# Token-mixing MLP on one core: three pairs of unit blocks of the first product as seven block products over 12 of the 16 token rows, the half block first, early gelu results by way of DRAM

## The chip, the cores and the metric

The kernel runs on one NeuronCore of a Trainium2 chip. The metric is the device time of one execution in microseconds (us). Before the change three runs gave 671.99 us in the median (670.89 to 672.05). One further execution was recorded with a profile. Engines carry the profile's names: PE (TensorE, matmuls; PEld its weight loads), ACT (ScalarE), DVE (VectorE), POOL (GpSimd), SP (SyncE, which here issues nearly all DMAs). PSUM is the memory that PE writes its results to, SBUF the large on-chip memory.

## The reference

```python
h = _layernorm(x, axis=-1) * (1 + ca) + sa
x = x + ga * _A_ref(h, A_k, A_v, A_shift_k, A_ssm_k, A_ssm_D)   # short and long convolution along the tokens
h = _layernorm(x, axis=-1) * (1 + cb) + sb
# _B_ref(x, w1, b1, w2, b2): the MLP over the token axis
h = _layernorm(x, axis=-1)                     # (1, S=2048 tokens, D=640 channels)
u = jnp.einsum("bsd,sf->bdf", h, w1) + b1      # F=1728 hidden units
u = _gelu(u)
y = jnp.einsum("bdf,fs->bds", u, w2) + b2
x = x + gb * y                                 # y back in (1, S, D)
```

All data are fp32. The change lies in the first product, `u = gelu(w1^T h + b1)`.

## The kernel before

**Stages.** Up to about 290 us the kernel computes the convolution half. Then comes the MLP. The 2048 tokens lie as 16 rows `j` of 128 partitions, each with 640 channels; the 1728 units are 13 blocks of 128 and a half block of 64 (f = 13). fp32 accuracy on fp32r matmuls takes three products: a value is split into a high part (`H[j][0]`) and the rest (`H[j][1]`), a weight block likewise, and `mm` (L439) issues high x high, high x rest, rest x high, each for the two halves of 320 channels. A block is thus 16 rows x 3 steps x 2 halves = 96 matmuls of 128x320.

**Norm and products.** The loop over row pairs `pr` (0 to 7) normalises two rows (`root_in`, `root`, `halves`, `rests`, `norm1`, `second`) and multiplies them with unit blocks 0 to 3 (`products`, L784), which fill all four PSUM tiles.

**The other blocks.** Blocks 4 to 12 follow one after another (L957). `load_w` (L396) fetches a block ahead over SP, `split_w` (L424) makes its two parts on ACT (L434) and DVE, alternating between `wb0b` and `wb1b`. `u_evac` (L872) takes a finished PSUM tile: gelu in place on ACT (L877), then for each half an ACT copy of the high part (L887) and a DVE subtraction for the rest. The half block comes between blocks 5 and 6 (`half_block`, L908): plain fp32 on whole rows that `whole_rows` adds up again from high part and rest. All gelu results `U` stay in SBUF.

**The second product.** Its first four row blocks use the plain form (L1119, `U[0]` to `U[13]` in order). Twelve more are made pairwise as seven block products instead of eight (Winograd's form of Strassen's scheme; L1042). `t_ops` (L919) prepares sums of `U` for it; `t_ops(0)` to `t_ops(2)` stand ahead of `u_evac(12)`.

**What sets the order.** Each engine runs its instructions in the order in which the program text issues them. `psum()` hands out four tiles of 1024 fp32 (two halves of 512, of which 320 are used) in a ring; `mem(tag, n, name)` gives the SBUF region `tag` to a new use. Waits between engines are derived from what overlaps by a framework; DMAs of SP rotate through eight semaphores, so at most eight are outstanding.

Of the kernel before, what the change touches and what calls it, by code (L numbers as in the profile page):

```python
# [47 lines left out]
def mixer_kernel(ctx: ExitStack, tc: tile.TileContext, q, k, v, shift_k, ssm_k, ssm_D, w1, b1, w2, b2, c,  # L48
# [8 lines left out]
    TT = lambda eng, o, a, b, op: eng.tensor_tensor(o, a, b, op=op)  # L57
# [366 lines left out]
    def split_w(n, t2=None, eng=dve):  # L424
        if n >= len(order):
            return
        i = order[n]
# [4 lines left out]
        t, parts = raw.pop(i)
        for f in parts:
            act.activation(hi[:, f].bitcast(F32R), t[:, f], AF.Copy)  # L434
# [427 lines left out]
    U = {}  # L862
    thirds = lambda t, n, o=0: [t[:, o + 320 * i:o + 320 * i + 320] for i in range(n)]
    h_i, h_y = mem("in", 4288, "h_i"), mem("y", 4096, "h_y")
# [5 lines left out]
    us = [home(left[2 * f:2 * f + 2], right[2 * f:2 * f + 2]) for f in range(6)]  # L870

    def u_evac(f, ps):  # L872
        n = 25 - f if f > 11 else f
        u = U[f] = us[n] if n < 13 else [t[:, 320 * h:320 * h + 320] for t in H[15] for h in range(2)]
        if f < 13:
            p = [ps[:, h, 0:320] for h in range(2)]
            act.activation(ps[:, :, 0:320], ps[:, :, 0:320], AF.Gelu_apprx_tanh, bias=B1C[:, f:f + 1])  # L877
        else:
            p = [ps[64:128, 1, 0:320], ps[64:128, 0, 0:320]]
            for h in range(2):  # L880
                r = slice(64 * h, 64 * h + 64)
                act.activation(p[h], ps[r, 0, 0:320], AF.Gelu_apprx_tanh, bias=B1C[r, f:f + 1])
            for t_ in u:
                dve.memset(t_[0:64], 0.0)
            u = [t_[64:128] for t_ in u]
        for h in range(2):
            act.activation(u[h].bitcast(F32R), p[h], AF.Copy)  # L887
# [2 lines left out]
    m_p = mem("p", 2048, "m_p")
    HALF = 6
    w_half = m_p[:, 0:1024].rearrange("p (j m) -> p j m", j=16)
    whole = [t[:, 640 * i:640 * i + 640] for t, n in ((h_i, 6), (h_y, 6), (m_p[:, 1024:1664], 1)) for i in range(n)]
    whole = [(t[:, 0:320], t[:, 320:640]) for t in whole] + [(h_i[:, 3840:4160], m_p[:, 1664:1984])]
    whole += whole[0:2]

    def whole_rows(js):
        for j in js:  # L900
            if j != 13:
                o = whole[j][0]
                TT(dve, bass.AP(tensor=o.tensor, offset=o.offset, ap=[o.ap[0], [1, 640]]), *H[j], ALU.add)
            else:
                for h in range(2):
                    TT(dve, whole[j][h], *(t[:, 320 * h:320 * h + 320] for t in H[j]), ALU.add)

    def half_block(ps):  # L908

        for j in range(16):  # L910
            if j == 2:
                whole_rows((14, 15))
            for h in range(2):
                pe.matmul(ps[64 * h:64 * h + 64, 0, 0:320], w_half[:, j], whole[j][h], start=j == 0, stop=j == 15)  # L914
# [34 lines left out]
    T_wb = [mem("w0", 4096, "wb0b"), mem("w1", 4096, "wb1b")]
    u_evac(0, acc[0])  # L950
    split_w(4)
    load_w(5)
    for b in range(2):
        sync.dma_start(w_half[64 * b:64 * b + 64], dram(w1, 16 * b * F + 1664, [[32 * F, 64], [F, 16], [1, 64]]))
    for f_ in range(1, 4):
        u_evac(f_, acc[f_])
    for f_ in range(4, NF - 1):  # L957
        if f_ == HALF:
            ps = psum().rearrange("p (h m) -> p h m", h=2)
            half_block(ps)  # L960
            u_i, u_y = mem("in", 4288, "u_i"), mem("y", 4096, "u_y")
            us.append(home((thirds(u_i, 1, 3840) + thirds(r_z, 1, 7680)), right[12:14]))
            us += [thirds(t, 4, 1280 * i) for t in (u_i, u_y) for i in range(3)]
            u_evac(13, ps)
        ps = psum().rearrange("p (h m) -> p h m", h=2)
        split_w(f_ + 1)
        load_w(f_ + 2)
        if f_ < HALF:
            whole_rows(range(7 * f_ - 28, 7 * f_ - 21))
        for j in range(16):  # L970
            hh, hl = H[j]
            mm(ps, blk[f_][0][:, j], blk[f_][1][:, j], hh, hl, j == 0, j == 15)
        if f_ == NF - 2:
            m_v = mem("v", 4520, "m_v")
            for i in range(3):
                t_ops(i)
        u_evac(f_, ps)
# [210 lines left out]
```

## Time and profile before

| | |
|---|---|
| median of three runs | 671.99 us (670.89 to 672.05) |
| the profiled execution's own time | 675.24 us |
| its span (first to last instruction in the trace) | 673.5 us |
| mean granted TensorE clock | 0.98 |
| PE's share of the span | 93% |
| product loop for blocks 0 to 3, half block, blocks 4 to 12 | about 298 to 490 us |
| second product, plain form | 490 to 539 us |
| second product, seven products for a pair | 539 us to the end |

The trace lists each group of instructions as start, duration, engine, source line, operation, output<-inputs, shapes, count, and in brackets how long the engine stood idle ahead of it and who released it. Matmul ends are modelled; starts are recorded. 1.74 us of the execution lie outside the span (675.24 - 673.5).

### The profile page before, as it was taken

How to read it: one execution, taken by the hardware profiler on the slowest of the kernel's cores; microseconds unless marked ns; L12 is line 12 of the kernel's file. 1: busy time of each engine (PE TensorE's matmuls, PEld its weight loads, DVE VectorE, ACT ScalarE, POOL GpSimd, SP SyncE). 2: the span in 40 equal slices, each digit the busy share in tenths (PEclk: the TensorE clock that was granted, in tenths of full speed). 3: DMA queues.
4: the chain of work that ended last, by engine and by line, in shares of the span. 5: the costliest groups of instructions: out<-in, count | busy, mean ns of one | idle time of the engine just before them, and what ended most of it. 6: DMA issues, size and time to landing. Idle time of an engine off the chain costs nothing.

```text
span 673.5 us, 20730 instructions
## 1 busy us (share of the span) xinstructions
PE 628.8 (93%) x9115; PEld 597.2 (89%) x9115; DVE 498.5 (74%) x869; ACT 300.7 (45%) x483; POOL 127.1 (19%) x142
## 2 busy tenths in 40 slices
PE   6868878899999999879999999999999999999997
PEld 2868578889998997779899889999999999999997
DVE  7788778969899269789966622321589869888895
ACT  0564465736747456377764222322344143333331
POOL 5772038424126044000000000000000430000000
PEclk9999979999999799789999999999999999999999
DMA  9998998456525234160307433335342626346601
GB/s 177 217 242 232 319 178 165 103 88 144 98 66 178 66 98 151 33 141 19 63 1 130 90 64 63 63 63 118 113 134 68 195 80 184 116 138 168 187 33 38
DMA packets 166537, 81.22 MB, mean 121 GB/s; under 512 B 90830, under 2 KB 156912, under 8 KB 166448
## 3 DMA queue, kind: packets, MB, share of 16 engines
q1 hardware_dynamic: 159276, 78.32, 47.8%
q10 hardware_dynamic: 6916, 1.31, 1.2%
q8 instruction: 71, 1.16, 0.8%
q0 software_dynamic: 256, 0.28, 0.2%
q14 instruction: 18, 0.15, 0.1%
HBM read 69.40 MB, written 10.49 MB: 119 GB/s over the span
## 4 chain that ended last, share of the span: by engine, by line
PE 69%; DVE 16%; DMA 7%; issue 3%; ACT 3%; SPq 2%; ACTq 0%; DVEq 0%
PE pst L445 22%; PE pst L1042 16%; PE pst L1119 7%; PE pst L223 7%; PE pst L242 6%; PE pst L271 5%; PE pst L291 3%; DVE p L57 3%; DMA p<-in_w_mod_dram 2%; DMA in<-in_A_v_dram 2%; DMA v<-in_const_v_dram 1%; ACT z L280 1%; DVE tap L57 1%; PE pst L914 1%; DVE sm L548 1%
## 5 line engine op out<-in xcount | busy, mean ns | idle before, releaser
L242 PE MATMUL pst<-z,w 128*64 128x64 f32 x2560 | 78.6, 223 | 12.8 <-DVE p L57 6.6
L242 PEld LDWEIGHTS pst<-z,w 128*64 128x64 f32 x2560 | 76.5, 138 | 15.4 <-issue 11.0
L229 ACT ACTIVATE z<-pst 128x1024 f32<-128x1024 f32 (+2 forms) x45 | 43.0, 973 | 41.6 <-PE pst L223 41.5
L57 POOL TENSOR_TENSOR y<-p 128x256 f32<-128x256 f32 x72 | 51.3, 740 | 42.4 <-DVE p L57 42.1
L57 DVE TENSOR_TENSOR p<-pst,kt 128x512 f32<-128x512 f32 x80 | 50.9, 687 | 8.3 <-ACT kt L246 8.3
L57 POOL TENSOR_TENSOR m_p<-u_i,r_z 128x320 f32<-128x320 f32 x1 | 0.9, 874 | 263.9 <-DVE m_p L57 263.9
L271 PEld LDWEIGHTS pst<-v,y 32*128 32x128 f32 x1280 | 39.5, 192 | 5.4 <-issue 5.0
L271 PE MATMUL pst<-v,y 32*128 32x64 f32 x1280 | 41.5, 278 | 2.3 <-issue 2.2
L877 ACT ACTIVATE pst<-pst,sm 128x640 f32<-128x640 f32 x13 | 10.0, 766 | 71.6 <-PE pst L445 71.6
L1042 PE MATMUL pst<-r_z,m_w 128*128 128x320 f32 x222 | 41.6, 309 | 0.1
L223 PE MATMUL pst<-v,p 128*64 128x128 f32 x640 | 38.4, 281 | 1.9 <-ACT p L168 1.9
L246 ACT ACTIVATE kt<-pst 128x512 f32<-128x512 f32 x40 | 23.9, 598 | 34.6 <-PE pst L242 20.0
L223 PEld LDWEIGHTS pst<-v,p 128*64 128x64 f32 x640 | 36.4, 142 | 3.2 <-ACT p L168 2.7
L1030 ACT ACTIVATE m_w<-m_v 128x896 fp32r<-128x896 f32 x24 | 22.7, 951 | 31.5 <-PE pst L1042 16.8
L57 DVE TENSOR_TENSOR tap<-tap,kt 128x512 f32<-128x512 f32 x51 | 35.6, 697 | 1.3
L223 PE MATMUL pst<-v,x 128*64 128x128 f32 x512 | 34.4, 292 | 2.0 <-issue 1.5
L1042 PEld LDWEIGHTS pst<-r_z,m_w 128*128 128x128 f32 x222 | 34.8, 188 | 0.4 <-DVE m_w L57 0.4
L223 PEld LDWEIGHTS pst<-v,x 128*64 128x64 f32 x512 | 31.0, 147 | 3.2 <-issue 2.5
L291 PEld LDWEIGHTS pst<-z,v 64*64 64x64 f32 x1280 | 24.2, 157 | 9.0 <-issue 5.1
L280 ACT ACTIVATE z<-pst 128x512 f32<-128x512 f32 x38 | 20.9, 642 | 24.6 <-PE pst L271 24.6
L291 PE MATMUL pst<-z,v 64*64 64x64 f32 x1280 | 25.8, 242 | 6.1 <-issue 3.8
L57 DVE TENSOR_TENSOR m_w<-m_v,m_w 128x896 fp32r<-128x896 f32 x24 | 27.9, 1165 | 2.5 <-ACT m_w L1030 2.1
(306 smaller groups left out, 1496.0 us busy)
## 6 DMA issues: line engine op xcount, KB each, us to landing
x<-in_B_w_dram SPq DMA_DIRECT2D x20, 512.0 KB
m_x<-xs SPq DMA_DIRECT2D x28, 160.0 KB
out_dram<-m_x SPq DMA_DIRECT2D x28, 160.0 KB
aux<-in_A_ssm_k_dram SPq DMA_DIRECT2D x8, 512.0 KB
m_v<-in_B_w_dram SPq DMA_DIRECT2D x9, 448.0 KB
in<-in_w_mod_dram SPq DMA_DIRECT2D x4, 960.0 KB
x<-in_B_w_dram SPq DMA_DIRECT2D x7, 448.0 KB
in<-in_A_v_dram SPq DMA_DIRECT2D x22, 128.0 KB
```

Source lines behind the costliest of these rows:

```text
L57: TT = lambda eng, o, a, b, op: eng.tensor_tensor(o, a, b, op=op)
L223: pe.matmul(ps[64 * ri:64 * ri + 64, o:o + 255:2], lhs, F1[:, 128 * ri:128 * ri + 128], start=True, stop=True)
L229: act.activation(Z[:, side, t, :, k0:k1], ps.rearrange("p (a k e) -> p a k e", a=4, e=2)[:, :, k0:k1], AF.Copy)
L242: pe.matmul(ps[64 * h:64 * h + 64, o:o + 64], W2[k1 // 32][:, 2 * (k1 % 32) + ri], rhs, start=True, stop=True)
L246: act.activation(kt.rearrange("p (m i) -> p m i", i=32), pv[:, :, 1], AF.Copy)
L271: pe.matmul(pp[qd // 2][:, o:o + 64], Y[p, ri, i:i + 2].rearrange("p i k -> p (i k)"), V2[p, 64 * ri:64 * ri + 64], start=ri == 0, stop=ri ...
L280: act.activation(o, i, AF.Copy)
L291: pe.matmul(ps[64 * b:64 * b + 64, 512 * e + 64 * jj:512 * e + 64 * jj + 64], V1[p, ri, n2], T2[p, :, 32 * ri + n2], start=ri == 0, stop=r ...
L445: pe.matmul(ps[0:m, h, 0:320], w_.bitcast(F32R), r_[:, 320 * h:320 * h + 320].bitcast(F32R), start=first and i == 0, stop=last and i == 2)
L1030: act.activation(W[n][0].bitcast(F32R), A[p, w_], AF.Copy)
L1042: pe.matmul(bank[n], w[:, i].bitcast(F32R), r.bitcast(F32R), start=i == 0 and k == 0, stop=i == 6 and k == 2)
L1119: pe.matmul(acc[s][:, h, 0:320], w[:, f_].bitcast(F32R), u[r + h].bitcast(F32R), start=f_ == 0 and k == 0, stop=f_ == NF - 1 and k == 2)
```

## The change

Blocks 5 to 10 become three pairs. For a pair, 12 of the 16 rows form a two by two scheme: unit blocks f and f + 1; row groups `KA` (rows 0 to 3, 8, 9) and `KB` (rows 10 to 15); two halves of 320 channels. It is made as seven block products (`p_prod`: A11, A12, S1, S2, S4, S3, A22) of 6 rows x 3 steps = 18 matmuls. The remaining rows `KR` (4 to 7) take four plain products (`r_prod`) of 4 x 3 = 12. A pair is thus 7 x 18 + 4 x 12 = 174 matmuls in place of 192. Each product fills one half of a PSUM tile: a and b are the halves of one tile, c_ and d those of a second.

Around it: `fulls(pr)` keeps the normalised rows themselves (12 ACT operations of 128x640 in the product loop), since `x_sums` (12 DVE operations) builds sums of rows from them, and `x_parts` splits those (12 ACT copies, 13 DVE subtractions); for S3 and A22 this is done in `turns()` inside the first pair. Each weight tile (6 or 4 rows of w1) is loaded, summed (`w_sum`) and split (`w_parts`) by itself. The half block moves ahead of block 4. `U[0]` to `U[4]` and the row `GB` are written to DRAM (`away`, 21 DMAs) and fetched back ahead of the weights of the second product. Blocks 4, 11 and 12 keep the old form; `u_evac` and `t_ops` keep theirs too.

```diff
+    def fulls(pr):
+        for j in (2 * pr, 2 * pr + 1):
+            act.activation(row(j), row(j), AF.Identity, scale=at(R_, 2, j))
@@ product loop
+        if pr != 4:
+            fulls(pr - 2 if pr < 4 else pr - 1)
         rests(pr)
         products(pr)
@@ after it
+    def w_parts(key, t, hi, lo):
+        Ws[key] = hi, lo
+        act.activation(hi.bitcast(F32R), t, AF.Copy)
+        TT(dve, lo.bitcast(F32R), t, hi, ALU.subtract)
+    def w_split(p, w_, n=None):
+        w_parts((p, w_), tile_of(p, w_), *SL[(7 * p + (TYPES.index(w_) if n is None else n)) % 2])
+    def r_split(p, n):
+        w_parts((p, "R%d" % n), RT[2 * (p % 2) + n - 1], *RH)
+    half_ps = psum().rearrange("p (h m) -> p h m", h=2)
+    js = (0, 1, 10, 11, 2, 3, 12, 13, 8, 9, 4, 5, 6, 7, 14, 15)
+    for j in js:
+        for h in range(2):
+            pe.matmul(half_ps[64 * h:64 * h + 64, 0, 0:320], w_half[:, j], whole[j][h], start=j == js[0], stop=j == js[-1])
+    w_0 = mem("w0", 4096, "s_w0")
...
+            u = thirds(w_0, 4, 1280 * n)
+            u_evac(n + 1, acc[n + 1], u)
+            away(n + 1, u)
...
+    for p in range(3):
+        f = 5 + 2 * p
+        banks = [psum() for _ in range(2)]
+        a, b, c_, d = (t[:, 512 * h:512 * h + 320] for t in banks for h in range(2))
...
+        p_prod(a, p, "A11")
+        act.activation(v_, a, AF.Copy)
+        if p:
+            w_split(p, "A12")
+            w_sum(p, "S1")
+        r_prod(b, p, 1, 0, True, False)
+        w_split(p, "S1")
+        p_prod(b, p, "A12", False)
+        w_sum(p, "S3")
+        w_sum(p, "S2")
+        w_load(p + 1, "A11")
+        TT(dve, b, v_, b, ALU.add)
+        if p:
+            gelu(f, raws[f][0], b)
+        w_split(p, "S2")
+        w_sum(p, "S4")
+        w_load(p + 1, "A12")
+        p_prod(c_, p, "S1")
+        r_prod(d, p, 1, 1, True, False)
+        if p == 0:
+            x_r = turns()
+            gelu(f, raws[f][0], b)
+        w_split(p, "S4")
+        w_load(p + 1, "A21")
+        r_split(p, 2)
+        p_prod(a, p, "S2")
+        TT(dve, u_, a, v_, ALU.add)
+        TT(dve, v_, c_, u_, ALU.add)
+        w_split(p, "S3")
+        w_load(p + 1, "A22")
+        p_prod(d, p, "S4", False)
+        TT(dve, d, v_, d, ALU.add)
+        gelu(f, raws[f][1], d)
+        r_prod(b, p, 2, 1, True, True)
+        w_split(p, "A22")
...
+        p_prod(a, p, "S3")
+        TT(dve, u_, a, u_, ALU.add)
+        TT(dve, v_, c_, u_, ALU.add)
+        TT(dve, b, v_, b, ALU.add)
+        gelu(f + 1, raws[f + 1][1], b)
+        r_prod(d, p, 2, 0, True, False)
...
+        p_prod(d, p, "A22", False)
+        TT(dve, d, u_, d, ALU.add)
+        gelu(f + 1, raws[f + 1][0], d)
...
+    for f in range(5):
+        U[f] = us[f]
+        away(f, us[f], True)
...
+    load_w(13)
+    part(1, "2", ps, last=True)
```

The order in which PE's instructions stand shows what takes the place of a block. Before, block 6 reads (one row stands for several equal matmuls, given by the count at its end; `wb0b` holds the block's weight parts, `r_z`, `r_v`, `h_a` and `h_x` the rows' parts, `pst_127` is the PSUM tile):

```order
L445 MATMUL pst_127_5370<-r_z_4273,wb0b_5062 128x320 [waits Activation_49]
L445 MATMUL pst_127_5370<-r_z_4273,wb0b_5062 128x320 x17
L445 MATMUL pst_127_5370<-r_v_4274,wb0b_5062 128x320 x18
L445 MATMUL pst_127_5370<-h_a_4275,wb0b_5062 128x320 x12
L445 MATMUL pst_127_5370<-h_a_4275,wb0b_5062 128x320 [waits Activation_49]
L445 MATMUL pst_127_5370<-h_a_4275,wb0b_5062 128x320 x5
L445 MATMUL pst_127_5370<-r_z_4273,wb0b_5062 128x320 x18
L445 MATMUL pst_127_5370<-h_x_4879,wb0b_5062 128x320 x24
```

After, the second pair begins with A11 into half a of `pst_128` (the last 15 of its 18 matmuls are the first four rows here), then the first R product into half b of the same tile:

```order
L935 MATMUL pst_128_5554<-r_z_4273,s_w0_5141 128x320 x6
L935 MATMUL pst_128_5554<-r_v_4274,s_w0_5141 128x320 x3
L935 MATMUL pst_128_5554<-h_a_4275,s_w0_5141 128x320 x3
L935 MATMUL pst_128_5554<-r_z_4273,s_w0_5141 128x320 x3
L935 MATMUL pst_128_5554<-r_v_4274,s_w0_5141 128x320 [waits Activation_49]
L935 MATMUL pst_128_5554<-r_v_4274,s_w0_5141 128x320
L935 MATMUL pst_128_5554<-r_v_4274,s_w0_5141 128x320 [waits DVE_49]
L935 MATMUL pst_128_5554<-r_v_4274,s_w0_5141 128x320 x3
L935 MATMUL pst_128_5554<-h_a_4275,s_w0_5141 128x320 x6
```

Further on in the same pair, the end of S2 (into a), S4 (into d of `pst_129`) and the second R product (into b of `pst_128`) stand so:

```order
L935 MATMUL pst_128_5554<-r_z_4273,s_w0_5141 128x320
L935 MATMUL pst_128_5554<-h_i_5269,s_w0_5141 128x320 x4
L935 MATMUL pst_129_5555<-r_z_4273,s_w0_5141 128x320 [waits DVE_49,Activation_49]
L935 MATMUL pst_129_5555<-r_z_4273,s_w0_5141 128x320 x5
L935 MATMUL pst_129_5555<-h_x_4883,s_w0_5141 128x320 x12
L935 MATMUL pst_128_5554<-r_v_4274,s_w0_5141 128x320 [waits Activation_49]
L935 MATMUL pst_128_5554<-r_v_4274,s_w0_5141 128x320 x5
```

Where one block ran through with one wait at its head, products of 12 or 18 matmuls now alternate between halves of two tiles, and the first matmul of each waits. `Activation_49` and `DVE_49` are counters of work that ACT and DVE have finished. The first wait of R1 is for the ACT copy of a to `v_`, that of S4 also for the DVE addition `v_ = c_ + u_`, which stands behind `u_ = a + v_`.

DVE, the first pair, from the low part of S1 to the low parts of S4 and R2 (`s_w_5072` holds weight tiles, `s_w_5141` their parts, `pst_5303` is the tile of a and b):

```order
L57 TENSOR_TENSOR s_w_5072<-s_w_5072 128x768
L57 TENSOR_TENSOR s_w_5072<-s_w_5072 128x768 [waits DVE_49]
L57 TENSOR_TENSOR pst_5303<-sm,pst_5303 128x320 [waits PE_49]
L57 TENSOR_TENSOR s_w_5141<-s_w_5072,s_w_5141 128x768 [waits Activation_49]
L57 TENSOR_TENSOR s_w_5072<-s_w_5072 128x768
L57 TENSOR_TENSOR r_v<-t_g,h_y 128x640 [waits Activation_49]
L57 TENSOR_TENSOR l_r<-t,h_y 128x640 [waits Activation_49]
L57 TENSOR_TENSOR l_g<-xb,h_y 128x640 [waits DVE_49,Activation_49]
L57 TENSOR_TENSOR l_g<-xb,h_y 128x640 [waits Activation_49]
L57 TENSOR_TENSOR l_t<-xb,h_y 128x640 [waits DVE_49,Activation_49]
L57 TENSOR_TENSOR l_t<-xb,h_y 128x640 [waits Activation_49]
L57 TENSOR_TENSOR s_w_5141<-s_w_5072,s_w_5141 128x768 [waits PE_49,Activation_49]
```

ACT at the same place: behind the six copies of `turns()` stands the gelu that reads b (L885) and writes to `x_r`, the region out of which `turns()` reads its last rows:

```order
L1052 ACTIVATE sm<-pst_5303 128x320 [waits PE_49]
L919 ACTIVATE s_w_5141<-s_w_5072 128x768 [waits DVE_49,Activation_49]
L919 ACTIVATE s_w_5141<-s_w_5072 128x768 [waits DVE_49,PE_49,Activation_49]
L956 ACTIVATE h_y<-t_g 128x640
L956 ACTIVATE h_y<-t 128x640
L956 ACTIVATE h_y<-xb 128x640 x4
L885 ACTIVATE x_r<-pst_5303,sm 128x320 [waits DVE_49]
```

Neither list has a counterpart before, where DVE and ACT between two blocks hold only the split of a weight block and an `u_evac`. On SP, the weights of block 13 (`load_w(13)`, L392 and L394) used to stand behind those of block 12:

```order
L403 DMA x<-in_B_w_dram 64x16x128 [waits DMAHW6_49,DVE_49]
L403 DMA x<-in_B_w_dram 64x16x128 [waits DMAHW7_49]
L392 DMA x<-in_B_w_dram 128x7x128 [waits DMAHW1_49,DMAHW0_49,DVE_49]
L392 DMA x<-in_B_w_dram 128x6x128 [waits DVE_49]
L394 DMA x<-in_B_w_dram 128x128
```

Now they stand behind the 20 DMAs that bring `U` back from `aside`, of which these are the last:

```order
L894 DMA u_x<-aside 128x320 [waits DMAHW7_49]
L894 DMA u_k<-aside 128x320 [waits DMAHW0_49]
L894 DMA u_x<-aside 128x320 [waits DMAHW1_49]
L894 DMA u_k<-aside 128x320 [waits DMAHW2_49]
L894 DMA u_x<-aside 128x320 [waits DMAHW3_49]
L392 DMA x<-in_B_w_dram 128x7x128 [waits DMAHW4_49]
L392 DMA x<-in_B_w_dram 128x6x128 [waits DMAHW5_49,DVE_49]
L394 DMA x<-in_B_w_dram 128x128 [waits DMAHW6_49]
```

More of the change, by code (lines that the diff above doesn't have):

```diff
@@ L860, in mixer_kernel @@
             load_w(4)
[L862 to L864 removed]
+        if pr == 5:
+            w_half = mem("p", 2048, "w_p")[:, 0:1024].rearrange("p (j m) -> p j m", j=16)
+            for b in range(2):
+                sync.dma_start(w_half[64 * b:64 * b + 64], dram(w1, 16 * b * F + 1664, [[32 * F, 64], [F, 16], [1, 64]]))
+    fulls(7)
+    U, raws, us, Ws = {}, {}, {}, {}
@@ new lines, in mixer_kernel, with u_parts, gelu, u_evac @@
+    thirds = lambda t, n, o=0: [t[:, o + 320 * i:o + 320 * i + 320] for i in range(n)]
+    aside = drp.tile([768, 1280], F32, name="aside")
+    def u_parts(f, raw, u):
+        U[f] = u
+        for h in range(2):
+            act.activation(u[h].bitcast(F32R), raw[h], AF.Copy)
+            TT(dve, u[2 + h].bitcast(F32R), raw[h], u[h], ALU.subtract)
+    def gelu(f, o, i):
+        act.activation(o, i, AF.Gelu_apprx_tanh, bias=B1C[:, f:f + 1])
+    def u_evac(f, ps, u):
+        gelu(f, ps[:, :, 0:320], ps[:, :, 0:320])
+        u_parts(f, [ps[:, h, 0:320] for h in range(2)], u)
@@ new lines, in away @@
+    def away(f, u, back=False):
+        for n, t in enumerate(u):
+            d = dram(aside, 128 * f * 1280 + 320 * n, [[1280, 128], [1, t.shape[-1]]])
+            sync.dma_start(*((t, d) if back else (d, t)))
+    K_OF = {"1": ((0, 4), (8, 2)), "2": ((10, 6),), "R": ((4, 4),)}
+    KA, KB, KR = [[j for a, n in K_OF[k] for j in range(a, a + n)] for k in "12R"]
+    tiles = lambda t, o, n: t[:, o:o + 128 * n].rearrange("p (j m) -> p j m", j=n)
+    TYPES = ("A11", "A12", "S1", "S2", "S4", "S3", "A22")
@@ new lines, in three_ @@
+    def three_(o, i, w, r, first, last):
+        for k, (w_, r_) in enumerate(((w[0][:, i], r[0]), (w[0][:, i], r[1]), (w[1][:, i], r[0]))):
+            pe.matmul(o, w_.bitcast(F32R), r_.bitcast(F32R), start=first and k == 0, stop=last and k == 2)
+    hp = lambda j, h: [t[:, 320 * h:320 * h + 320] for t in H[j]]
+    VA = [r_g, T_t, T_x[1][:, 0:1280]]
+    VB = [T_x[1][:, 1280 * i:1280 * i + 1280] for i in range(1, 4)]
+    quad = lambda v, h: v.rearrange("p (j h d) -> p j h d", j=2, h=2)[:, :, h]
@@ new lines, in p_prod, with r_prod @@
+    def p_prod(o, p, w_, first=True):
+        for i in range(6):
+            three_(o, i, Ws[p, w_], MOV[w_](i), first and i == 0, i == 5)
+    def r_prod(o, p, n, h, first, last):
+        for i in range(4):
+            three_(o, i, Ws[p, "R%d" % n], hp(KR[i], h), first and i == 0, last and i == 3)
+    w_0, w_1 = mem("w0", 4096, "wh_w0"), mem("w1", 4096, "s_w1")
+    E = [tiles(w_1, 768 * i, 6) for i in range(5)]
+    whole = {j: [row(j)[:, 320 * h:320 * h + 320] for h in range(2)] for j in (*KA, *KB)}
@@ new lines, in mixer_kernel @@
+    for i, j in enumerate(KR):
+        whole[j] = thirds(w_0, 2, 640 * i)
+        TT(dve, w_0[:, 640 * i:640 * i + 640], *H[j], ALU.add)
+    for w_ in ("A11", "A12"):
+        w_load(0, w_)
+    u = thirds(w_0, 4, 2560)
+    u_evac(0, acc[0], u)
+    away(0, u)
+    for w_ in ("A21", "A22"):
+        w_load(0, w_)
+    split_w(4, mem("y", 4096, "wb4"))
+    for n in (1, 2):
+        w_load(0, "R%d" % n)
+    away(5, [GB])
+    half_ps = psum().rearrange("p (h m) -> p h m", h=2)
+    js = (0, 1, 10, 11, 2, 3, 12, 13, 8, 9, 4, 5, 6, 7, 14, 15)
@@ new lines, in mixer_kernel @@
+    ps4 = psum().rearrange("p (h m) -> p h m", h=2)
+    for j in range(16):
+        mm(ps4, blk[4][0][:, j], blk[4][1][:, j], *H[j], j == 0, j == 15)
+    h_i, l_p, l_k = mem("in", 4288, "h_i"), mem("p", 2048, "l_p"), mem("kt", 1536, "l_k")
+    x_parts("S1", h_i[:, 0:1920], [[t] for t in piece(l_p, 3)])
+    u = thirds(w_0, 4, 2560)
+    u_evac(3, acc[3], u)
+    away(3, u)
+    w_split(0, "A11")
+    r_split(0, 1)
+    x_parts("S2", h_i[:, 1920:3840], [[t] for t in piece(l_k, 2)] + [thirds(r_z, 1, 7680) + thirds(h_i, 1, 3840)])
@@ new lines, in mixer_kernel, with turns @@
+    w_split(0, "A12")
+    w_sum(0, "S1")
+    h_y, l_r = mem("y", 4096, "h_y"), mem("rows", 640, "l_r")
+    v_, u_ = thirds(sm, 2, 41)
+    def turns():
+        lo = [[r_v[:, 3840:4480]], [l_r], None]
+        x_parts("S3", h_y[:, 0:1920], lo, (0, 1))
+        l_g, l_t = mem("g", 1280, "l_g"), mem("t", 1280, "l_t")
+        g_, t_ = piece(l_g, 2), piece(l_t, 2)
+        lo[2] = [g_[0]]
+        x_parts("S3", h_y[:, 0:1920], lo, (2,))
+        x_parts("A22", h_y[:, 1920:3840], [[g_[1]], [t_[0]], [t_[1]]])
+        x_r = mem("xb", 5120, "x_r")
+        raws[13] = thirds(x_r, 2)
+        for f in range(5, 10):
+            raws[f] = thirds(x_r, 2, 640 * (f - 4))
+        return x_r
@@ L865, in mixer_kernel @@
+    w_split(3, "A12")
+    m_p = mem("p", 2048, "m_p")
+    act.activation(m_p[:, 0:1280], x_r[:, 640:1920], AF.Copy)
+    u_y = mem("y", 4096, "u_y")
+    for n in range(3):
+        us[10 + n] = thirds(u_y, 4, 1280 * n)
+    u_parts(9, raws[9], us[9])
+    u_parts(13, raws[13], us[12])
+    GB = mem("rows", 640, "gb")
+    away(5, [GB], True)
     left = [t_ for t, n in ((mem("t", 1280, "u_t"), 4), (mem("g", 1280, "u_g"), 4), (mem("kt", 1536, "u_k"), 4))
             for t_ in thirds(t, n)]
-    u_x = mem("xb", 5120, "u_x")
@@ L868, in mixer_kernel @@
-    right = thirds(u_x, 14)
+    right = thirds(mem("xb", 5120, "u_x"), 14)
     home = lambda l, r: [l[0], r[0], l[1], r[1]]
[L870 to L888, printed above, removed]
@@ L892, in mixer_kernel @@
[L892 to L906, printed above, removed]
@@ L908, in half_block @@
[L908 to L914, printed above, removed]
+    for f in range(6):
+        us[f] = home(left[2 * f:2 * f + 2], right[2 * f:2 * f + 2])
+    us[6] = home(thirds(u_i, 1, 3840) + thirds(r_z, 1, 7680), right[12:14])
+    for f in range(5):
+        U[f] = us[f]
+        away(f, us[f], True)
@@ L947, in t_ops @@
         rest(3, a)
[L949 to L977, printed above, removed]
+    ps = psum().rearrange("p (h m) -> p h m", h=2)
+    part(1, "1", ps, first=True)
+    w_split(3, "A21", 2)
+    for f in (5, 6):
+        u_parts(f, [m_p[:, 640 * (f - 5) + 320 * h:640 * (f - 5) + 320 * h + 320] for h in range(2)], us[f])
+    part(1, "R", ps)
+    r_split(3, 2)
+    load_w(13)
+    part(1, "2", ps, last=True)
+    w_split(3, "A22", 3)
+    u_evac(11, ps, us[11])
+    T_wb = [w_0, mem("w1", 4096, "wb1b")]
+    split_w(13)
+    load_w(14)
+    ps = psum().rearrange("p (h m) -> p h m", h=2)
+    for k in "1R2":
+        part(2, k, ps, k == "1", k == "2")
+    m_v = mem("v", 4520, "m_v")
+    for i in range(3):
+        t_ops(i)
+    u_evac(12, ps, [t[:, 320 * h:320 * h + 320] for t in H[15] for h in range(2)])
     NP = 6
```

78 lines of the change are left out of this document (76 added, 2 removed).

## Prediction

> **What bounds the kernel now.** I read first the busy times, then the windows by stage.
>
> ```profile
> PE 628.8 (93%) x9115; PEld 597.2 (89%) x9115; DVE 498.5 (74%) x869; ACT 300.7 (45%) x483; POOL 127.1 (19%) x142
> 295.00:300.00 5.00, 2.34 (x10) 2.08 (x10) 4.76 (x13) 3.81 (x9) 0.00 (x0) 0.80 0.13 26
> 300.00:305.00 5.00, 5.00 (x31) 5.00 (x31) 4.93 (x10) 4.20 (x6) 0.00 (x0) 0.85 0.43 105
> 305.00:354.00 49.00, 46.72 (x314) 45.86 (x313) 42.35 (x104) 35.03 (x64) 0.00 (x0) 1.00 0.11 23
> 354.00:382.00 28.00, 28.00 (x193) 28.00 (x192) 19.16 (x28) 9.44 (x15) 0.00 (x0) 1.00 0.66 120
> 391.00:489.00 98.00, 98.00 (x669) 97.90 (x668) 30.75 (x46) 27.23 (x41) 0.00 (x0) 1.00 0.39 85
> 490.00:537.00 47.00, 47.00 (x322) 47.00 (x321) 43.88 (x75) 16.88 (x29) 8.27 (x6) 1.00 0.42 121
> ```
>
> A window row gives the stretch, its length, busy time and count of PE, PEld, DVE, ACT and POOL, the granted PE clock, and DMA share and rate. From 354 us on PE is busy throughout at full clock, while DVE works 30.75 of 98 us and ACT 27.23. In the stage that changes, PE alone sets the time: every matmul less is worth its pace, and every wait of PE costs its whole length. In the product loop (305 to 354) PE idles 2.28 us, and DVE and ACT are nearly full.
>
> **What is saved.**
>
> ```profile
> 368.17 2.80 PE L445 MATMUL pst<-r_z,wb1b 128*128 128x320 f32 x18
> 370.81 2.80 PE L445 MATMUL pst<-r_v,wb1b 128*128 128x320 f32 x18
> 382.34 3.45 PE L914 MATMUL pst<-h_i,m_p 128*64 128x320 f32 x24
> 539.07 1.04 PE L1042 MATMUL pst<-u_t,m_w 128*128 128x320 f32 x6
> 539.95 1.04 PE L1042 MATMUL pst<-u_g,m_w 128*128 128x320 f32 x6
> ```
>
> 18 matmuls start within 370.81 - 368.17 = 2.64 us: 0.1467 each. The rows of L1042, where as in the new products only one half is written at a time, give 0.88 / 6, the same. Three pairs times 192 - 174 = 18 matmuls are 54 less: **-7.92 us**. The half block moves and keeps its work (3.45 us for the first 24 of its matmuls): nothing.
>
> **What PE waits for: the release of a PSUM tile.**
>
> ```profile
> 349.81 0.44 ACT L887 ACTIVATE u_t<-pst 128x320 fp32r<-128x320 f32 x1
> 350.27 0.49 DVE L57 TENSOR_TENSOR u_t<-pst,u_t 128x320 fp32r<-128x320 f32 x1 [2.98 <-ACT u_t L887]
> 350.80 0.44 ACT L887 ACTIVATE u_x<-pst 128x320 fp32r<-128x320 f32 x1 [0.56 <-DVE u_t L57]
> 545.43 0.44 ACT L1061 ACTIVATE m_x<-pst 128x320 f32<-128x320 f32 x1 [1.06 <-PE pst L1042]
> ```
>
> In `u_evac` the ACT copy of the second half (350.80) waited 0.56 us for DVE's read of the first (350.27 to 350.76): the program orders accesses of different engines by the whole tile, not by its halves. In the order after the change, PE's first matmul into one half waits likewise for the reader of the other. A pair has places where a product's predecessor, into the same tile, must first drain (a matmul lasts 0.31 modelled, less 0.147 until the next start: 0.16) and be read:
> - R1 into b, behind A11 into a: `v_` copy 0.44 and a handover of 0.05 (349.81 + 0.44 to 350.27 gives 0.02, DVE to ACT 0.04): 0.65.
> - S4 into d, behind S2: two DVE additions, `u_` and then `v_`, which reads c_, d's neighbour. 0.16 + 2 x 0.49 + 0.10 = 1.24, if DVE is free.
> - R2 into d, behind S3: `u_` reads S3's a, then `v_` reads c_ again: 1.24. (The R2 before it goes into b, whose tile nobody reads then.)
>
> DVE is not always free at S4. S2 can start at the end of its own low part; behind that DVE sums S4, waits for ACT's copy of it, and makes the low parts of S4 and R2.
>
> ```profile
> 365.84 2.29 DVE L57 TENSOR_TENSOR h_i<-r_z 128x640 f32<-128x640 f32 x3
> 478.99 2.09 DVE L57 TENSOR_TENSOR wb1b<-x,wb1b 128x896 fp32r<-128x896 f32 x2 [0.35 <-ACT wb1b L434]
> L877 ACT ACTIVATE pst<-pst,sm 128x640 f32<-128x640 f32 x13 | 10.0, 766 | 71.6 <-PE pst L445 71.6
> L434 ACT ACTIVATE wb1b<-x 128x896 fp32r<-128x896 f32 x2 | 1.8, 945 | 0.0
> L57 DVE TENSOR_TENSOR m_p<-m_p 128x320 f32<-128x320 f32 x12 | 5.9, 492 | 0.4
> ```
>
> The last three rows are groups: busy time, mean ns of one. No row has 768 or 512 elements a partition; I interpolate: 0.82 at 640 and 1.09 at 896 (from 2.29 / 3 with its overlap, and 2.09 / 2) give 0.95 for 768 and 0.66 for 512 on DVE, 0.86 on ACT. From the end of S2's low part: 0.95 + (0.86 + 0.05) + 0.95 + 0.6 = 3.4 us until DVE reaches `u_`; S2 itself takes 18 x 0.1467 + 0.16 = 2.80. The two additions start 0.6 to 0.7 late: 1.9 instead of 1.24. Pairs 2 and 3 thus cost 0.65 + 1.9 + 1.24 = 3.8 each, **+7.6**.
>
> In the **first pair** `turns()` hides the S4 delay in a larger one. S2 goes into a, whose neighbour b is read by `gelu(5)`; ACT has that behind all six copies, and it writes to the region that `turns()` still reads. From the end of A12 DVE does: sum for S2 0.95, the addition to b 0.49, S2 low 0.95, S4 sum 0.95, six subtractions of 640 (spaced by 2.29 / 3, 0.75, so 4.5); then gelu 0.49 (as the 320-wide DVE operation; 0.766 is for 640) and handovers: 8.8 us. PE meanwhile has S1 (18 matmuls) and R1 into d (12): 4.4. Wait: **+4.4**. S4 and R2 then cost 1.24 each, **+2.5**. R1's wait is longer here, since `v_` stands behind ACT copies that themselves wait until `U[3]`, lying where R1's weight parts go, has been stored: 0.65 plus half a DMA's time, **+1.3** (from 0.65 to 3).
>
> Block 4's tile is that of block 1's result. Its `u_evac` writes into `w_0`, which the half block's last rows occupy: drain, two copies, two subtractions and handovers are 0.16 + 0.88 + 0.98 + 0.15 = 2.2; the half block's last two rows (four matmuls of 3.45 / 24 x 2, some 1.1) cover half: **+1.1**.
>
> **The product loop.**
>
> ```profile
> 331.91 1.55 ACT L777 ACTIVATE r_z<-xb,kt 128x640 fp32r<-128x640 f32 x2 [1.46 <-DVE kt L749]
> 330.15 0.30 ACT L740 ACTIVATE kt<-kt,sm 128x4 f32<-128x4 f32 x1 [0.67 <-DVE kt L721]
> 337.60 0.30 ACT L740 ACTIVATE kt<-kt,sm 128x2 f32<-128x2 f32 x1
> 338.25 0.16 DVE L746 RECIPROCAL kt<-kt 128x2 f32<-128x2 f32 x1
> ```
>
> A pair of `fulls` costs ACT what a pair of `halves` does, 1.55. Ahead of the square root at 330.15 ACT had 0.67 us to spare, ahead of the one at 337.60 none; DVE took that result 0.35 us after its end (338.25 - 337.90). So one of the six pairs delays the chain root, `halves`, PE by 1.55 - 0.35 = **+1.2**. Bounds: 0, if ACT catches up, and 3.1, if two pairs count.
>
> **The results stored away.**
>
> ```profile
> 488.97 0.91 SPq L1000 DMA_DIRECT2D m_v<-xs  x2
> 533.15 3.67 SPq L1000 DMA_DIRECT2D m_x<-xs  x8
> 534.00:535.00 1.00, 1.00 (x9) 1.00 (x8) 0.97 (x2) 0.00 (x0) 1.00 (x1) 1.00 0.95 264
> 535.00:536.00 1.00, 1.00 (x9) 1.00 (x9) 1.00 (x1) 0.00 (x0) 0.36 (x1) 1.00 0.96 287
> 481.00 0.49 DVE L57 TENSOR_TENSOR m_p<-u_t 128x320 f32<-128x320 f32 x1
> 499.13 0.49 DVE L57 TENSOR_TENSOR h_x<-pst,h_x 128x320 fp32r<-128x320 f32 x1 [0.50 <-ACT h_x L887]
> 500.33 1.04 PE L1119 MATMUL pst<-h_x,wb1b 128*128 128x320 f32 x6
> 489.76 0.31 PE L1119 MATMUL pst<-u_t,wb1b 128*128 128x320 f32 x1
> ```
>
> Before, `t_ops(0)` to `(2)` began at 481.00 and `u_evac(12)` ended at 499.62, 18.6 later and 0.71 before PE needed it at 500.33, 10.6 after that stage's start (489.76). Now the same chain hangs on the fetches. Counted from the start of block 11: about 5.2 until all that reads `x_r` is through (drain, addition, gelu and a split copy 2.0; a copy of 1280 elements 1.4; four copies spaced 0.45). Then 20 fetches of 160 KB, issued every 0.47 us (8.9 for 19), but 3.3 MB: where the trace has eight such fetches in a row (533.15), 16 queues were 95% busy at 264 and 287 GB/s, and so 20 take 12. Behind them the 0.9 MB of `load_w(13)`, 3.3; the split of its last half, 2.0; then 18.6: 41.1 in all. PE needs it after 192 x 0.1467 + 10.6 = 38.8: late by 2.3. [...] Bounds: 0, if issue and not transfer sets the pace (38.0 in all), and 8, if transfers run at three quarters of that rate (16 and 4.4).
>
> **The sum.** -7.92 + 7.6 + 4.4 + 2.5 + 1.3 + 1.1 + 1.2 + 3.0 = **+13.2**. One thing is added.
>
> ```profile
> 298.24 5.82 PE L445 MATMUL pst<-r_z,wb 128*128 128x320 f32 x28 [2.66 <-DVE aux L57]
> ```
>
> After an idle time of 2.66 us, 28 matmuls took 5.82 instead of 4.11, the windows show clocks of 0.80 and 0.85: 1.7 us lost. The wait of 4.4 should bring that too, **+1.7** (0, if only longer ones do; 5, if those of 1.9 do it as well). So +14.9: 675.24 becomes 690.1 on the profiled execution's footing. That execution stood 3.25 above the median; on the median's footing, the one I predict, **671.99 + 14.9 = 686.9**.
>
> **The rivals.**
> - *The waits are by bank, not by tile*, the faster side. Speaks for it: the halves lie 512 elements apart and 320 are used, so no data overlap. [...] Against: the wait at 350.80 and the program's order, which has it written in. Then 7.6, 4.4, 2.5 and R1's 1.3 go, and the clock's 1.7: -7.9 + 1.1 + 1.2 + 3.0 = -2.6, 669.4. It decides wherever the reader of the other half ends later than PE's own work. Chance 0.05.
> - *The change does only what it says*: all side work hidden, 671.99 - 7.9 + 1 = 665. It needs DVE and ACT to be idle where PE asks. They are half idle in the windows, but not at the points counted above. Chance 0.03.
> - *The fetch comes later still*: 8 instead of 3 and 1.7 for another loss of clock, 693.6. Speaks for it: the trace has no row of 20 fetches. Against: DMA is idle for much of the windows there (share 0.39). Chance 0.15.
> - *Half the waits*: DVE's 768-wide operations at 0.8 and handovers hidden: S4 1.24, S2 3; and the fetch at 1: some 6 us less, 681. Chance 0.15. About no change needs waits of 8 instead of 21 in sum: 0.02.
>
> **How the numbers follow.** My forecast has 0.60. The range holds it and most of the two near rivals, 680 to 694; the ends of the single bounds (fulls 3.1, clock 5, R1 3) lie within it unless two come together. 0.2% (1.3 us) is about what a measurement of this kernel can tell from no change. Faster by more: 0.08 (both fast rivals). Within it: 0.02. Slower: 0.90.
>
> **What would show it.** In the profile after: PE idle ahead of the first matmul of R1, S4 and R2 with ACT or DVE as releaser, 0.65, 1.2 to 1.9 and 1.24; one wait of 4 to 5 us ahead of the first pair's S2, released by ACT's gelu, with a clock under 1.00 behind it; matmuls fewer by 54 (9061); a wait ahead of the matmuls of `U[12]`. If PE runs through the three pairs without idle time, the prediction is wrong in its main term; if the waits are there but the loss at `U[12]` is large, the rival of the fetch holds.

## The result

The changed kernel takes 690.95 us in the median of six runs (688.38 to 697.30), the kernel before 672.02 (six runs, 668.97 to 672.97): ratio 1.0301, 95% interval 1.0250 to 1.0353, slower by 18.9 us between the medians. The forecast was 686.9 (680.0 to 694.0), slower by 14.9.

PE's timeline of the changed kernel, rows with idle time only: start, duration, engine, line, operation, count, and in brackets the idle time ahead and who ended it.

```profile
337.17 14.68 PE L445 MATMUL pst<-h_x,wb 128*128 128x320 f32 x96 [0.78 <-ACT h_x L778]
361.65 2.91 PE L445 MATMUL pst<-r_z,wb 128*128 128x320 f32 x18 [1.03 <-DVE s_w L57]
379.36 1.15 PE L935 MATMUL pst<-r_v,s_w 128*128 128x320 f32 x6 [0.72 <-ACT sm L1052]
392.77 0.41 PE L935 MATMUL pst<-h_i,s_w 128*128 128x320 f32 x1 [4.33 <-ACT x_r L885]
398.42 1.11 PE L935 MATMUL pst<-r_z,s_w 128*128 128x320 f32 x6 [1.20 <-DVE sm L57]
406.89 1.12 PE L935 MATMUL pst<-r_v,s_w 128*128 128x320 f32 x6 [1.20 <-DVE sm L57]
414.69 1.16 PE L935 MATMUL pst<-r_v,s_w 128*128 128x320 f32 x6 [0.53 <-ACT sm L1052]
428.21 1.12 PE L935 MATMUL pst<-r_z,s_w 128*128 128x320 f32 x6 [1.80 <-DVE sm L57]
436.67 1.11 PE L935 MATMUL pst<-r_v,s_w 128*128 128x320 f32 x6 [1.20 <-DVE sm L57]
444.46 1.14 PE L935 MATMUL pst<-r_v,s_w 128*128 128x320 f32 x6 [0.53 <-ACT sm L1052]
458.00 1.67 PE L935 MATMUL pst<-r_z,s_w 128*128 128x320 f32 x6 [1.82 <-DVE sm L57]
468.01 1.11 PE L935 MATMUL pst<-r_v,s_w 128*128 128x320 f32 x6 [1.20 <-DVE sm L57]
515.23 0.41 PE L1329 MATMUL pst<-h_x,wb1b 128*128 128x320 f32 x1 [3.87 <-ACT h_x L881]
516.22 1.69 PE L1329 MATMUL pst<-h_x,wb1b 128*128 128x320 f32 x5 [0.58 <-ACT h_x L881]
```

The waits stand where the forecast put them and come close to its sizes: `v_` copy 0.53, `u_` and `v_` 1.20, S4 1.80, the first pair's S2 4.33, released by the gelu (L885). None is in the trace of before, where PE has no idle time behind the product loop. The rows behind three of them are slow: six matmuls take 1.67 instead of 1.11 at 458.00.

The busy times, and four windows (length; PE, PEld, DVE, ACT, POOL; granted PE clock; DMA share, GB/s):

```profile
PE 628.2 (91%) x9061; PEld 592.2 (86%) x9061; DVE 537.3 (78%) x930; ACT 328.6 (48%) x534; POOL 128.4 (19%) x143
393.00:398.00 5.00, 4.22 (x18) 3.96 (x17) 2.27 (x4) 1.81 (x3) 0.00 (x0) 0.66 0.25 69
458.00:463.00 5.00, 5.00 (x24) 5.00 (x25) 1.21 (x2) 0.02 (x1) 0.00 (x0) 0.66 0.62 155
510.00:515.00 5.00, 1.35 (x10) 1.09 (x8) 4.58 (x11) 2.80 (x6) 0.00 (x0) 1.00 0.04 14
515.00:520.00 5.00, 4.19 (x16) 3.86 (x17) 3.91 (x7) 2.29 (x4) 0.00 (x0) 0.66 0.09 24
```

There are 9115 - 9061 = 54 matmuls less, as the change says, and DVE has 39 us more to do, ACT 28. The clock is at 0.66 over five us at three places; at each, 11 to 18 matmuls lose 1.5 to 1.7 us (S2's 18 of the first pair took from 392.77 to 398.42 - 1.20, 4.45 us instead of 2.80).

The part of the program ahead of the change varies by up to 8 us from one execution to the next (the matmuls at 298.24 before start at 290.90 to 299.26 in the other profiles). Profiles are therefore compared from one matmul of the product loop to the end of the span: before 673.5 - 332.79 = 340.7, after 690.5 - 329.07 = 361.4, **+20.7** (one execution each; the medians differ by 18.9).

```profile
329.07 7.33 PE L445 MATMUL pst<-r_z,wb 128*128 128x320 f32 x48 [0.76 <-ACT r_z L778]
```

### The profile page after: what moved, and what is told of

It is laid out like the page before. It is cut to its first block, busy times and chain, and to the rows that moved or that the text cites. A ratio compares the mean times of both kernels' runs of the same rounds, so it can differ in the third digit from the quotient of the medians.

```text
span 690.5 us, 20938 instructions
## 1 busy us (share of the span) xinstructions
PE 628.2 (91%) x9061; PEld 592.2 (86%) x9061; DVE 537.3 (78%) x930; ACT 328.6 (48%) x534; POOL 128.4 (19%) x143
## 4 chain that ended last, share of the span: by engine, by line
PE 54%; DVE 24%; DMA 6%; ACT 6%; issue 4%; SPq 4%; ACTq 0%; POOL 0%; DVEq 0%; POOLq 0%
PE pst L1252 16%; PE pst L935 8%; PE pst L223 8%; PE pst L271 6%; PE pst L1329 6%; PE pst L242 5%; DVE p L57 3%; PE pst L291 2%; DVE tap L57 2%; DVE s_w L57 2%; SPq L894 2%; DVE aux L57 1%; PE tap L351 1%; DVE kt L57 1%; PE pst L994 1%
## 5 line engine op out<-in xcount | busy, mean ns | idle before, releaser
L57 DVE TENSOR_TENSOR s_w<-s_w,s_w 128x768 fp32r<-128x768 f32 x25 | 23.9, 957 | 30.5 <-ACT s_w L919 25.7
L271 PEld LDWEIGHTS pst<-v,y 32*128 32x128 f32 x1280 | 41.1, 201 | 3.4 <-issue 2.9
L271 PE MATMUL pst<-v,y 32*128 32x64 f32 x1280 | 43.0, 287 | 0.3 <-issue 0.2
L223 PE MATMUL pst<-v,p 128*64 128x128 f32 x640 | 36.9, 274 | 3.2 <-ACT p L168 1.8
L223 PEld LDWEIGHTS pst<-v,p 128*64 128x64 f32 x640 | 34.8, 137 | 4.8 <-ACT p L168 2.8
L445 PE MATMUL pst<-r_z,wb 128*128 128x320 f32 x180 | 29.7, 322 | 5.3 <-DVE aux L57 2.7
L445 PEld LDWEIGHTS pst<-r_z,wb 128*128 128x128 f32 x180 | 28.2, 198 | 6.7 <-DVE aux L57 2.9
L919 ACT ACTIVATE s_w<-s_w 128x768 fp32r<-128x768 f32 x25 | 21.0, 840 | 21.1 <-DVE s_w L57 12.7
L57 DVE TENSOR_TENSOR kt<-in,tap 128x512 f32<-128x512 f32 x42 | 28.8, 685 | 1.2
```

Source lines behind the costliest of these rows:

```text
L223: pe.matmul(ps[64 * ri:64 * ri + 64, o:o + 255:2], lhs, F1[:, 128 * ri:128 * ri + 128], start=True, stop=True)
L271: pe.matmul(pp[qd // 2][:, o:o + 64], Y[p, ri, i:i + 2].rearrange("p i k -> p (i k)"), V2[p, 64 * ri:64 * ri + 64], start=ri == 0, stop=ri ...
L445: pe.matmul(ps[0:m, h, 0:320], w_.bitcast(F32R), r_[:, 320 * h:320 * h + 320].bitcast(F32R), start=first and i == 0, stop=last and i == 2)
L919: act.activation(hi.bitcast(F32R), t, AF.Copy)
```

## The experiments

"Stage" is the time from that matmul row to the end of the span, against the 340.7 of before; ratios are timed runs against the kernel before on the same chip. e2 and e19 ran on another chip than e1, e3, e7 and e17, so ratios are compared and not times.

| run | ratio (95% interval) | stage, us against before |
|---|---|---|
| the change | 1.0301 (1.0250 to 1.0353) | +20.7 |
| e1_tiles | 1.0145 (1.0092 to 1.0197) | +9.0 |
| e3_w13_first | 1.0215 (1.0165 to 1.0264) | +14.7 |
| e7_fill | 1.0280 (1.0236 to 1.0323) | +20.1 |
| e2_u12_first | 1.0320 (1.0269 to 1.0371) | +15.2 |
| e17_all | 0.9913 (0.9881 to 0.9945) | -4.0 |
| e19_fulls | 0.9946 (0.9915 to 0.9977) | -5.1 |

**Other tiles for the pairs (e1_tiles).**

```diff
-        banks = [psum() for _ in range(2)]
-        a, b, c_, d = (t[:, 512 * h:512 * h + 320] for t in banks for h in range(2))
+        t_a = psum()
+        b = half_ps[:, 1, 0:320] if p == 0 else psum()[:, 0:320]
+        d = psum()[:, 0:320]
+        a, c_ = t_a[:, 0:320], t_a[:, 512:832]
```

> Only the PSUM homes of the pairs change: a and c_ share a tile, b and d get tiles of their own (in the first pair b takes the free half of the half block's tile). If the waits come from accesses being ordered by the whole tile, the seven waits of the second and third pair (0.53, 1.80, 1.20 and 0.53, 1.82, 1.20 us) and R1's 0.72 go, also the first pair's two of 1.20, and the 1.7 us that the low clock at 458 us cost; the wait of 4.33 does not go: it moves from S2 to S4, whose weight copy stands on ACT behind the gelu of b (about 4.2). Sum 690.95 - 7.1 - 0.7 - 2.4 - 1.7 = about 679, ratio to before 1.011. Rival: DVE and ACT set the pace of a pair, and the waits only move to the next product that needs them: no more than 2 us less, ratio 1.027 to 1.03.

All waits of PE in its timeline from the half block to the end of the third pair:

```profile
366.49 2.90 PE L445 MATMUL pst<-r_z,wb 128*128 128x320 f32 x18 [1.03 <-DVE s_w L57]
398.36 2.43 PE L935 MATMUL pst<-r_z,s_w 128*128 128x320 f32 x6 [3.37 <-ACT s_w L919]
418.01 0.86 PE L935 MATMUL pst<-r_z,s_w 128*128 128x320 f32 x4 [0.21 <-DVE s_w L57]
444.50 0.86 PE L935 MATMUL pst<-r_z,s_w 128*128 128x320 f32 x4 [0.20 <-DVE s_w L57]
```

Eight waits of 0.53 to 1.82 are gone, with the same work on DVE and ACT (537.2 and 329.1 us busy, in the change 537.3 and 328.6); two of 0.2 have come. The first pair's 1.20 ahead of S4 is now part of the large wait. The waits were the ordering by the whole tile, not a lack of DVE time: the rival falls. The large wait moved to S4, as expected, and is 3.37 there: ACT's copy of S4's weights stands behind the gelu of b, which waits for `turns()`. The expected ratio, 1.011, lies within the measured interval. The wait at `U[12]` stayed (2.73 and 0.37 us), and the clock was low for longer at each of the two large waits: 0.78 and 0.54 over the five us from 395 and from 400, 0.70 and 0.61 from 505 and from 510, where the change has 0.66 over five us once at each place.

**Weights ahead of the fetches (e3_w13_first).**

```diff
-    for f in range(5):
-        U[f] = us[f]
-        away(f, us[f], True)
     u_parts(10, raws[10], us[10])
...
     load_w(13)
+    for f in range(5):
+        U[f] = us[f]
+        away(f, us[f], True)
```

> Only the order on SP changes: the 20 fetches of U stand behind load_w(13) instead of ahead of it. If the wait at U[12] (4.45 us, and 1.7 for the clock behind it) comes from that queue, both go: 690.95 - 6.1 = about 685, ratio 1.020, with the weights' split 5 us earlier against block 12. Rival: the lateness is DVE's own backlog (three t_ops ahead of U[12]), and the fetches, which t_ops need too, are then late in their place: wait of 3 us or more stays at U[12], ratio 1.027 to 1.03.

In the changed kernel, SP's queue (issues: start, time, line, count) and ACT's split of `load_w(13)` read:

```profile
477.78 0.32 SPq L894 DMA_DIRECT2D u_x<-aside  x1
481.59 2.47 SPq L894 DMA_DIRECT2D u_x<-aside  x1
488.37 0.43 SPq L894 DMA_DIRECT2D u_x<-aside  x1
488.85 1.08 SPq L392 DMA_DIRECT2D x<-in_B_w_dram  x2
494.74 0.95 ACT L434 ACTIVATE wb1b<-x 128x896 fp32r<-128x896 f32 x1 [5.32 <-DMA x<-in_B_w_dram]
496.08 0.95 ACT L434 ACTIVATE wb1b<-x 128x896 fp32r<-128x896 f32 x1 [0.40 <-DMA x<-in_B_w_dram]
```

From the second of them on (477.78), the fetches occupied SP for 11 us; one issue lasted 2.47 where the other 19 took 0.32 to 0.54, and no row names what held it. The first half of the weights was there 5.9 us after its issue, and ACT waited 5.32 for it. In DVE's order the low parts of these weights stand ahead of `t_ops`, and `t_ops` ahead of block 12's evacuation, so the whole chain slid. With the order on SP changed, ACT splits the weights without waiting:

```profile
494.15 1.78 ACT L434 ACTIVATE wb1b<-x 128x896 fp32r<-128x896 f32 x2
497.13 0.49 DVE L57 TENSOR_TENSOR m_p<-u_t 128x320 f32<-128x320 f32 x1
```

DVE's first operation of `t_ops` (497.13) now stands 8.3 us ahead of PE's first matmul of the second product (505.46), in the change only 2.55 (498.08 and 500.63). PE has no idle time at `U[12]`: stage 6.0 us less than the change's, against 6.1 expected; ratio 1.0215 against 1.020. The rival falls: the order of the queue was the cause, though it acted by way of DVE's order, as the next run shows.

**Block 12's evacuation first (e2_u12_first).** The same wait, approached from DVE's side.

```diff
-    for i in range(3):
+    for i in range(2):
         t_ops(i)
     u_evac(12, ps, [t[:, 320 * h:320 * h + 320] for t in H[15] for h in range(2)])
+    t_ops(2)
```

> Only one line moves: block 12's evacuation stands ahead of the third t_ops instead of behind it; the fetches stay ahead of load_w(13). In the changed kernel t_ops began at 498.08 and took 5.6 us each. With two of them ahead the evacuation can end at about 498.1 + 11.2 + 1.9 = 511.2, when PE asks for it at 511.3: the wait of 4.45 us and the clock's 1.7 go, to 685, ratio 1.020. Rival: DVE is so late by then that what is put off returns as waits of PE further on, at the first products of the second product's pairs (539 us before), which need all seven t_ops: 2 us or more of it come back, ratio 1.023 to 1.027.

The wait went from `U[12]` and came back, 2.05 us in all, at the next weight block, whose split on ACT and DVE stands behind the `t_ops` that was put off. The rival had expected it later, at the pairs:

```profile
509.80 0.42 PE L1330 MATMUL pst<-u_t,s_w 128*128 128x320 f32 x1 [1.77 <-ACT s_w L434]
510.93 0.42 PE L1330 MATMUL pst<-u_t,s_w 128*128 128x320 f32 x1 [0.28 <-DVE s_w L57]
```

In this profile, of the fastest of its four executions, the stage is 5.5 us shorter than the change's, 2.4 of that by the wait; the rest fits two falls of the clock that did not come, at `U[12]` and behind the third pair's wait (1.00 from 440 to 520). The timed runs (683.19 to 694.76) show no gain: the expected 1.020 lies below the interval, and the 1.032 can't be told from the change's 1.0301.

**PE kept busy during the wait (e7_fill).** 24 matmuls more, whose results nobody uses (`w_1[...] if 0 else RH[0][...]` is always `RH[0][...]`).

```diff
             gelu(f, raws[f][0], b)
+            for i in range(24):
+                pe.matmul(half_ps[:, 1, 0:320], w_1[:, 0:128].bitcast(F32R) if 0 else RH[0][:, 0].bitcast(F32R), hp(KR[0], 1)[0].bitcast(F32R), start=True, stop=True)
```

> 24 matmuls more (128x320, results unused, in the free half of the half block's tile) stand ahead of the first pair's S2, in the place of its wait of 4.33 us. They need 3.5 us. If the lower clock behind that wait (0.66 in the window from 393 us) is caused by PE's idle time, the wait shrinks to about 0.8 and the 1.7 us come back, though 24 matmuls are added: 690.95 - 1.7 = 689.2, ratio 1.0275, clock 1.00 in the five us behind. Rival: the low clock follows from something else (a fixed rhythm, or the rise of load at the start of the dense stretch): clock and time as without them, 691.

```profile
394.98 0.41 PE L935 MATMUL pst<-h_i,s_w 128*128 128x320 f32 x1 [0.83 <-ACT x_r L885]
393.00:398.00 5.00, 4.06 (x26) 3.53 (x25) 3.01 (x5) 2.01 (x4) 0.62 (x1) 1.00 0.12 35
428.00:433.00 5.00, 4.13 (x19) 4.16 (x20) 1.56 (x4) 0.00 (x0) 0.00 (x0) 0.71 0.65 165
```

The wait is 0.83, as expected, and the clock behind it 1.00 instead of 0.66: what was expected if PE's idle time is the cause at this place. The total hardly gained (stage 0.6 us shorter, 1.7 expected): this time the clock fell also behind the second pair's wait of 1.81 (0.71 from 428 to 433), where it had not in the change's profile (1.00 from 408 to 438), and at `U[12]` it was 0.55 from 515 to 520, in the change 0.66. By time, 1.0280 agrees with the 1.0275 expected, but can't be told from the change's 1.0301 either.

**All together (e17_all, e19_fulls).** e17 takes e1's tiles (with another tile for the second pair's a) and e3's order. In the first pair it puts the splits of S4 and R2 ahead of `turns()`, divides `turns()`, and moves R2's first product behind S3 and the evacuations of block 4 and the half block behind the next weights' split. In the half block, rows 4 to 7 come early. Parts of the edit:

```diff
-    js = (0, 1, 10, 11, 2, 3, 12, 13, 8, 9, 4, 5, 6, 7, 14, 15)
+    js = (0, 1, 4, 5, 6, 7, 10, 11, 2, 3, 12, 13, 8, 9, 14, 15)
...
-        if p == 0:
-            x_r = turns()
-            gelu(f, raws[f][0], b)
         w_split(p, "S4")
         w_load(p + 1, "A21")
         r_split(p, 2)
+        if p == 0:
+            l_ = turns()
...
         w_load(p + 1, "A22")
+        if p == 0:
+            x_r = turns2(*l_)
+            gelu(f, raws[f][0], b)
         p_prod(d, p, "S4", False)
```

> All that was found together: tiles as in e1 (with the second pair's a not in the half block's tile), in the first pair the splits of S4 and R2 ahead of turns(), turns() in two parts around S2's evaluation and R2's first product behind S3, the evacuation of block 4 and the half block behind the next weights' split, load_w(13) ahead of the fetches, and the rows 4 to 7 early in the half block, so that block 1's results can be written sooner. If the waits are these and nothing else, what is left is -7.9 + 0.8 (fulls) + about 2 of small waits: 672.0 - 5 = 667, ratio 0.993. Rival: side work of DVE and ACT in the pairs is too much in sum: then waits of 1 to 4 us stay somewhere, ratio 1.00 to 1.01.

Its waits behind the product loop, all of them up to the second product's pairs:

```profile
392.60 0.56 PE L935 MATMUL pst<-h_y,s_w 128*128 128x320 f32 x2 [0.24 <-DVE s_w L57]
395.37 1.16 PE L935 MATMUL pst<-r_v,s_w 128*128 128x320 f32 x6 [0.16 <-ACT x_r L885]
406.68 0.85 PE L935 MATMUL pst<-r_z,s_w 128*128 128x320 f32 x4 [0.20 <-DVE s_w L57]
433.08 0.85 PE L935 MATMUL pst<-r_z,s_w 128*128 128x320 f32 x4 [0.20 <-DVE s_w L57]
```

From one pair to the next it now takes 433.08 - 406.68 = 26.40 us, in the change 444.46 - 414.69 = 29.77, and two plain blocks took 2 x (368.17 - 354.09) = 28.16. DVE and ACT have as much to do as in the change (537.3 and 327.8 us busy), and the four waits add up to 0.80 us: the rival, too much side work, falls. This version is faster than before by 0.9% (0.9913, its interval below 1), as expected (0.993).

e19 also spreads the `fulls` of rows 8 to 13: one between `root_in` and `halves`, one behind `second`.

> The combined version, with the fulls of rows 8 to 13 spread: of each pair one stands between root_in and halves, where ACT waits for DVE anyway, and one behind second. If the wait of 0.78 us ahead of the last 96 matmuls of the product loop comes from a whole pair of fulls ahead of root_in, it falls to about 0.3, and the time to 0.9 us below that of the combined version: ratio 0.990. Rival: ACT is simply full in the loop, then the wait stays at 0.7 or more and the ratio at 0.991.

The wait of 0.78 ahead of the last 96 matmuls is gone altogether, more than expected; the stage is 1.1 us shorter than e17's. In time e17 and e19 cannot be told apart, and the 0.990 expected lies just below e19's interval: the gain of this last step is seen in the profile alone.

## Why the prediction was right, and where its size was off

Waits in the trace don't contain the 0.16 us of drain (until the last matmul ahead has ended) that the forecast counted in; it is added here.

| step of the forecast | forecast | measured |
|---|---|---|
| 54 matmuls less | -7.9 | -7.9 |
| second and third pair: R1, S4, R2 | +7.6 | 7.08 + 6 x 0.16 = 8.0 |
| first pair: S2 behind the gelu | +4.4 | 4.33 + 0.16 = 4.5 |
| first pair: S4, R2 | +2.5 | 2.40 + 0.32 = 2.7 |
| first pair: R1 (half a DMA's time in it was the author's estimate) | +1.3 | 0.72 + 0.16 = 0.9 |
| block 4 | +1.1 | 1.03 + 0.16 = 1.2 |
| `fulls` in the product loop | +1.2 | 1.4 (22.72 against 21.30 to the loop's end), 0.8 of it wait |
| `U[12]` | +3.0 | 3.87 + 0.58 + 0.3 = 4.8 |
| low clock | +1.7 | about 4.9 (three times) |
| sum | +14.9 | 20.5 of 20.7 |

- **Tiles.** The step that carried the forecast, that PE is held by the reader of the tile's other half, was right in place and nearly in size, and e1 shows the cause: other homes for the same products, and the waits are gone.
- **The first pair.** Right, too, including what hides behind it: taking the tile's wait away only moved it to S4 (3.37). It took e17's order to remove it. Which of its four edits did how much there was not measured apart.
- **`U[12]`.** Right in cause (e3), 1.8 too small in size. The fetches began in earnest where the forecast had them (477.78, 5.3 us after the start of block 11; forecast 5.2). From there to the second half of the weights it took 18.3 us (to 496.08), where the forecast had 12 + 3.3 and, on the way from late by 2.3 to the +3.0 of its sum, 0.7 more = 16.0. No run shows that 0.7, an estimate of the author's; in the change's trace the DMA share was 0.00 from the issue at 477.78 to 478.60, and 0.18 at 26 GB/s from there to 478.80. The transfers did not hold the 264 and 287 GB/s of the forecast's rows throughout: from 483 to 485 us, while SP stood at the issue of 2.47, the DMA share was 0.48 at 132 GB/s.
- **The clock.** Mis-sized most: the forecast charged one loss of 1.7, behind the wait of 4.4. It came three times; one was behind a wait of 1.82, which the forecast had only as the upper bound (5), and one at `U[12]`, which it had put into the rival of the late fetch. These two are 3.2 of the 5.8 us that the forecast lacks.
- **The rivals.** "By bank, not by tile", each half of a tile by itself, fell with the trace of the change. It is right in one respect: nothing but the order that the program derives from tiles held PE, since e1 and e17 write and read the same data without it. "The change does only what it says" and "Half the waits" fell. "The fetch comes later still" came true in part: the loss at `U[12]`, 4.8, lies between the 3.0 of the forecast and its 8, and the further loss of clock that it named did come.

## What to carry to other kernels

When a product is cut into smaller ones, each with a reader of its own, look at which results share a tile of PSUM: a saving of 18 matmuls a pair (2.6 us) was outweighed by 4 us of waits for a neighbour's reader, and by putting together two results that are read at the same time the waits went. The chain of side work is best listed in the order of each queue: a gelu behind sums of rows, or weights behind 20 fetches, cost PE 4.3 and 4.5 us here, while e17 does the same side work in another order with 0.8 us of waits. And price PE's idle time above its length, since some of these waits cost 1.5 to 1.7 us of clock besides.
